# Exp blocks as the weights of the values product, rsqrt as a power on GpSimd, and a new order of the stages, in a fused attention and two-layer kernel

## The chip, the cores and the metric

The kernel runs on one core of a Trainium2 chip. A core has a matrix engine (TensorE, PE in the profile; its weight loads are listed as PEld), VectorE (DVE), ScalarE (ACT), GpSimd (POOL) and SyncE (SP), which here only issues DMAs. Each engine works through its own instructions in order and waits on semaphores for the others. The metric is the device time of one execution in microseconds. Three runs of the kernel before took 408.49, 407.97 and 408.43 us, so its median is 408.43 us. The profile is one further execution.

## The reference

There are 8 batches of 12 heads with 448 positions and 64 features a head. q and k are divided by their root mean square and scaled by g, then attention, then a layer of 2048 units with the "snake" function, then a second layer back to 768:

```python
q_n, k_n = (rmsnorm(q, g_q), rmsnorm(k, g_k))
scores = scale * np.matmul(q_n, k_n.transpose(0, 1, 3, 2))
scores = scores - np.max(scores, axis=-1, keepdims=True)
attn = np.exp(scores)
attn = attn / (np.sum(attn, axis=-1, keepdims=True) + 1e-09)
x = np.matmul(attn, v)            # heads side by side: 3584 x 768
h = x @ w_in                      # 3584 x 2048
s = np.sin(alpha * h)
g = h + s * s / (alpha + 1e-09)
out = g @ w_out                   # 3584 x 768
```

The kernel leaves out the subtraction of the maximum, before and after the change.

## The kernel before

**Stages.** One batch is one stage, and the stages overlap: stage b does the norms, scores, exps and the values product of batch b, then the first product of batch b (`first_product`), and between its steps it does the second product of batch b-1 in small portions called fills (`second_product`, `fill`). After stage 7 the second product of batch 7 is all that is left.

**Chunks and tiles.** A batch's 12 heads are three chunks of four heads. A chunk's scores come in seven tiles (`scores`): four matmuls on four 64x64 quadrants of the array, 448 columns each, into one pair of PSUM banks, and one exp by ACT over 128x896 that writes a bf16 tile `expT`. Keys stand on the partitions, queries on the free axis.

**Order.** Nothing schedules this on its own. Each stage has a plan, a string of tokens, worked off from left to right (`STAGE_0`, `STAGE_1`, and `STAGE_N` for stages 2 to 7), and a second dictionary of tokens that are done beside the first product (`h_plan`). Every engine gets its instructions in the order of the tokens. The tokens, chunk number first: `l` load q and k (two DMAs on SP); `q` squares (by ACT in the first two chunks, else by GpSimd); `u` sum of squares on DVE; `r` one over the root, by a log and an exp on ACT; `g` fold g into q; `k` scale q or k to bf16 (`k30` is chunk 3, q); `t` turn it with two DMA transposes on SP, or `p` with TensorE; `S` a score tile; `V` loads of v; `W` and `O` loads of the weights; `F` or a digit are fills of the second product's current unit, `f` one of the next unit. Chunks 3 to 5 are those of the next batch, 6 and 7 those after it. A fill is two steps of `quadrants` (L538 to L561): eight matmuls on 64x64 quadrants.

**PSUM.** There are four bank pairs. A digit string beside each plan says which pair the next user takes; a user waits until the pair's last reader is done.

**Values product (`attend`, L385 to L441).** v (bf16) is the weight and the exp tile the moving operand, so the result comes out with features on the partitions, ready for the first product. The sums over keys come from matmuls with a weight of ones. Chunk 0 has `o` (ones, halved tiles of 64x32, L404) and `v` (values, 64x64, L416). Chunks 1 and 2 are done together on 64x32 tiles: `x` ones, `y` and `z` the even and odd features. Every tile streams 448 columns, or 224 in the halved ones. The sums are turned into reciprocals by ACT, a log and an exp (L423 to L425, L431, L432), those of chunk 0 are put in place by DVE (L429), and DVE multiplies (L440) into `xT`, the operand of the first product.

**First product (`first_product`, L460 to L496).** 16 row tiles of 128 by six contraction steps kt of 128, 448 columns each (L468), two row tiles to a bank pair. ACT takes the sine (L446), the square is by GpSimd for even tiles (L449) and by ACT for odd ones (L451), DVE adds (L454) into `g_sb` and frees the bank pair.

Of the kernel before, what the change touches and what calls it, by code (L numbers as in the profile page):

```python
# [17 lines left out]
try:  # L18
# [15 lines left out]
        "q000 u000 q010 G q011 q001 u010 g00 u011 r01 g01 D1 u001 k01 r00 k00 q11 u11 O00 q10 V00 p012 "  # L34
        "W01 q20 p00 g1 u10 r1 q21 u20 V01 g2 S4 V02 S k11 l3 k10 S1 S1 S4 W00 W02 S u21 r2 p1 L S2 S q31 "
        "S3 k21 q30 k20 D2 S S3 o3 l4 g3 S W10 W12 o1 o3 p2 u30 l5 S3 u31 S1 S W11 S4 v7 S S S q40 S S x5 "
        "y3 q41 u41 x1 g4 z4 u40 x1 r4 y4 O01 q50 z3 r3 O10 "
    ),
    "012311203203312021021302301231032103021321302",
    {-1: 'u50 O11 k30', 0: 'D4 k401', 1: 'k411', 2: 'q51', 3: 'k31 k400 u51', 5: 'k410', 7: 'g5 V12', 8: 't3 V10 V11 t4 l6 l7'},  # L40
# [3 lines left out]
        "4 r2 f f k20 1 f f 2 k21 S 1 q31 1 t2 S 1 S 2 S q30 2 S 2 S S 3 f S 3 S 1 f S 1 S 1 u31 2 l5 g3 "  # L44
        "S u30 o1 o6 1 r3 V10 2 S f q41 1 f 2 S 2 S 2 q40 S u41 1 v1 v1 S v3 V12 S k31 q50 v2 u40 S 2 S "
        "V11 g5 S z4 x7 y7 r4 z3 g4 k30 "
    ),
    "1320201203203013133213130101301231203123",
    {-1: 'u50 t3', 0: 'k41', 2: 'k40', 5: 'q51', 6: 'l6 t4', 8: 'u51 l7'},
# [3 lines left out]
        "f q40 f 1 f 2 q41 1 S 1 r2 5 f S f f S 2 S 1 u40 k20 1 k21 S 1 u41 1 S 2 S 1 q31 1 o7 1 f f 1 S "  # L53
        "t2 f 1 r4 S 2 f 1 l5 q30 S 3 S 1 u31 1 S 2 u30 g3 V10 S 2 S S k41 3 S v6 r3 k30 S k31 v1 S 2 V12 "
        "g4 2 S 2 S 2 q51 l6 S t3 z3 x7 y5 y2 z4 V11 "
    ),
    "01223131310312323203013012301021310231023",
    {-1: 'k40', 0: 't4', 2: 'q50', 3: 'u50', 4: 'u51 g5', 6: 'l7'},
)
LAST = "0123012"  # L60


def tokens_of(plan):

    return [t for word in plan.split() for t in ("F" * int(word) if word.isdigit() else [word])]
# [3 lines left out]
def kernel(  # L69
# [14 lines left out]

    nc = tc.nc
# [11 lines left out]
    NC = NP // 2  # L105
    SCALE = float(D) ** -0.5
# [8 lines left out]
    vpool = ctx.enter_context(tc.tile_pool(name="vpool", bufs=2))  # L115
    npool = ctx.enter_context(tc.tile_pool(name="norm", bufs=2))
    tpool = ctx.enter_context(tc.tile_pool(name="qkT", bufs=8))
    epool = ctx.enter_context(tc.tile_pool(name="expT", bufs=17))
    hpool = ctx.enter_context(tc.tile_pool(name="parts", bufs=1))
    rpool = ctx.enter_context(tc.tile_pool(name="rec", bufs=2))  # L120
    xpool = ctx.enter_context(tc.tile_pool(name="xT", bufs=1))
# [6 lines left out]

# [3 lines left out]
    upcoming = deque()  # L132
# [11 lines left out]
    qk, vb, norm = {}, {}, {}  # L144

    def strip(pp, hi):

        s = 2 * hi + pp
        return slice(s * 32, s * 32 + 32)

    def half_of(c, pp, hi):

        return pp ^ (hi, 1, 0)[c]

    def load_qk(ci, k_queue=nc.sync):

# [17 lines left out]
    def load_v(b, c):  # L174


        if b not in vb:
            vb[b] = vpool.tile([P, NP, NJ, D], BF16, tag="vb", name="vb")
        heads = v[b].rearrange("(n pp) (p j) d -> n pp p (j d)", pp=2, j=NJ)
        rows = vb[b].rearrange("p n j d -> p n (j d)")  # L180
        if c == 1:
            for r in range(2):
                nc.gpsimd.dma_start(out=rows[r * 64:r * 64 + 64, 1:4], in_=heads[1:4, 1 - r].rearrange("n p x -> p n x"))
        else:
            n = slice(0, 1) if c == 0 else slice(4, NP)
            nc.gpsimd.dma_start(out=rows[:, n], in_=heads[n].rearrange("n pp p x -> (pp p) n x"))
# [7 lines left out]

    load_qk(0, nc.scalar)
# [6 lines left out]
    ones = const.tile([P, D], BF16)  # L202
    nc.vector.memset(ones, 1.0)
    ones_row = const.tile([1, P], F32)
    nc.vector.memset(ones_row, 1.0)
    eps = const.tile([P, 1], F32)
    nc.vector.memset(eps, 1e-6)
    ident = const.tile([P, P], BF16)
# [11 lines left out]
    def spread_g():  # L220

        nc.gpsimd.tensor_mul(g_rows[:, 2], g_rows[:, 0], g_rows[:, 1])
        ps = bank_pair("gps")
        nc.tensor.matmul(ps[:, 0, :D], ones_row, g_rows[:, 2], start=True, stop=True)
        nc.vector.tensor_copy(gg[:, 0], ps[:, 0, :D])
        give_back(ps)

    def spread_alpha():

# [6 lines left out]
    def load_w_in(half, c):  # L236


        cols = slice(half * D_FF // 2, (half + 1) * D_FF // 2)
        rows = moe_w_in[c * 2 * P:(c + 1) * 2 * P, cols]  # L240
        nc.gpsimd.dma_start(out=w_in_sb[half][:, 2 * c:2 * c + 2],  # L241
                            in_=rows.rearrange("(p x) f -> p x f" if c else "(x p) f -> p x f", x=2))

    def load_w_out(hi, lo):
        src = moe_w_out.rearrange("(mt p) d -> p mt d", p=P)
        part = 2 * hi + lo
        mts = slice(part * MT // 4, (part + 1) * MT // 4)
        nc.gpsimd.dma_start(out=w_out_sb[:, mts], in_=src[:, mts])  # L248

    def keep_busy(n, rhs):  # L250


# [7 lines left out]
    def norm_tasks(ci):  # L260

        st = SimpleNamespace()
        early = ci <= NC
        st.ms = npool.tile([P, 2, 2 * NJ], F32, tag="ms", name="ms")
        st.inv, st.inv_ps, st.scaled = {}, [], 0
        st.sq, st.n = {}, None
# [5 lines left out]
        def square(w, heads=(0, 1)):  # L274
            if ci < 2:
                st.sq[w] = spare(2 * ci + w).rearrange("p (a d) -> p a d", d=D)
                rows = slice(heads[0] * NJ, (heads[-1] + 1) * NJ)
                nc.scalar.activation(st.sq[w][:, rows], qk[ci][:, w, rows], ACT.Square)  # L278
            else:
                st.sq[w] = npool.tile([P, 2 * NJ, D], F32, tag="sq", name="sq")  # L280
                nc.gpsimd.tensor_mul(st.sq[w], qk[ci][:, w], qk[ci][:, w])  # L281
# [10 lines left out]
        def rsqrt(ws=slice(0, 2)):  # L292
            ln = npool.tile([P, 2, 2 * NJ], F32, tag="inv", name="inv")
            inv = bank_pair("inv") if early else ln
            if early:
                st.inv_ps.append(inv)
            for w in range(2)[ws]:
                st.inv[w] = inv[:, w, :2 * NJ]
            nc.scalar.activation(ln[:, ws], st.ms[:, ws, :], ACT.Ln, scale=1.0 / D, bias=eps)
            nc.scalar.activation(inv[:, ws, :2 * NJ], ln[:, ws], ACT.Exp, scale=-0.5)  # L300

        def scale(w, heads=(0, 1)):
            eng = nc.vector if early else nc.gpsimd
# [20 lines left out]


# [18 lines left out]
        st.square, st.fold_g, st.reduce, st.rsqrt, st.scale = square, fold_g, reduce, rsqrt, scale  # L344
        st.transpose, st.pe_transpose = transpose, pe_transpose
        return st

    def scores(c, j, warm=0):

# [3 lines left out]
        for pp in range(2):  # L353
            for hi in range(2):
                qkt, r = qkT[2 * c + pp], slice(hi * 64, hi * 64 + 64)
                o = half_of(c % NC, pp, hi) * 64
                nc.tensor.matmul(sc[o:o + 64, hi, :S], qkt[r, 1, j * REST:(j + 1) * REST], qkt[r, 0, :],  # L357
# [5 lines left out]
    avs, recs = {}, {}  # L363
    presums = {}

    def add_tile(b):


        if b not in presums:
            presums[b] = SimpleNamespace(n=0, t=rpool.tile([P, 2, S], F32, tag="rec", name="rec"))  # L370
        s = presums[b]
        first = expT[b * NC, 0] if s.n == 0 else s.t
        s.n += 1
        nc.vector.tensor_add(s.t, first, expT[b * NC, s.n])

    def split_sum(b):

        s = presums[b]
        assert s.n == NJ - 1
        s.parts = [hpool.tile([P, 2, S], BF16, tag=f"part{i}", name="part") for i in range(2)]  # L380
        nc.vector.tensor_copy(s.parts[0], s.t)
        nc.vector.tensor_sub(s.parts[1], s.t, s.parts[0])
# [298 lines left out]
```

The softmax here doesn't subtract the row's maximum and nothing guards it: scores larger than these inputs give would overflow.

## Time and profile before

The profiled execution has a span of 405.8 us from the first to the last instruction; the median of the three timed runs, 408.43 us, is 2.6 us above it.

| | |
|---|---|
| median of three runs | 408.43 us (407.97 to 408.49) |
| span of the profiled execution | 405.8 us |
| stage 0, to the first matmul of a second product | 54.4 us |
| stage 1 | 45.5 us |
| stages 2 to 7, each | 46.8 to 46.9 us |
| after the last first product | 24.5 us |
| score exps on ACT (L360) | 168 x 917 ns |
| squares on GpSimd (L281) | 44 x 1678 ns |
| scaling on GpSimd (L309) | 80 x 938 ns |
| folding g on GpSimd (L286) | 23 x 2098 ns |

How to read it: the times of stages are cut where TensorE passes from line L468 (first product) to line L548 or L529 (second product). A matmul's length in the profile includes its way through the array, some 0.19 us, and consecutive matmuls overlap, so the cost of one in a stream is the distance between starts. "issue" is time in which an engine waited for nothing that the profile shows.

### The profile page before, as it was taken

How to read it: one execution, taken by the hardware profiler on the slowest of the kernel's cores; microseconds unless marked ns; L12 is line 12 of the kernel's file. 1: busy time of each engine (PE TensorE's matmuls, PEld its weight loads, DVE VectorE, ACT ScalarE, POOL GpSimd, SP SyncE). 2: the span in 40 equal slices, each digit the busy share in tenths (PEclk: the TensorE clock that was granted, in tenths of full speed). 3: DMA queues.
4: the chain of work that ended last, by engine and by line, in shares of the span. 5: the costliest groups of instructions: out<-in, count | busy, mean ns of one | idle time of the engine just before them, and what ended most of it. 6: DMA issues, size and time to landing. Idle time of an engine off the chain costs nothing.

```text
span 405.8 us, 15218 instructions
## 1 busy us (share of the span) xinstructions
PE 391.4 (96%) x6755; PEld 238.8 (59%) x6758; DVE 240.6 (59%) x364; ACT 315.3 (78%) x474; POOL 283.6 (70%) x268
## 2 busy tenths in 40 slices
PE   1999999999999999999999999999999999999996
PEld 1346467645675566755676556755667556765564
DVE  4956665756783576638584475836685485544512
ACT  5798889868896879958898678958898679877600
POOL 5998889987959789588877779597895784003300
PEclk9999999999999999999999999999999999999999
DMA  7999999855286925697076923879046901620022
GB/s 266 215 254 241 210 221 255 193 155 171 53 164 162 151 94 88 182 198 153 3 140 178 200 102 70 185 158 209 3 94 179 166 2 22 108 61 1 2 78 79
DMA packets 67846, 55.46 MB, mean 137 GB/s; under 512 B 41524, under 2 KB 63172, under 8 KB 67780
## 3 DMA queue, kind: packets, MB, share of 16 engines
q1 hardware_dynamic: 56578, 41.43, 42.2%
q0 software_dynamic: 10432, 11.81, 19.0%
q8 instruction: 53, 0.87, 0.9%
q10 hardware_dynamic: 770, 1.25, 0.9%
q14 instruction: 13, 0.11, 0.1%
HBM read 45.62 MB, written 11.01 MB: 140 GB/s over the span
## 4 chain that ended last, share of the span: by engine, by line
PE 88%; POOL 5%; DMA 3%; issue 1%; DVE 1%; ACT 1%; SPq 0%; POOLq 0%
PE hps L468 34%; PE ops L548 31%; PE av L416 9%; PE sc L357 7%; PE ops L529 5%; POOL sq L281 2%; DMA qk<-in_q_dram 2%; DMA qk<-in_k_dram 2%; PE av L404 1%; POOL qk L286 1%; POOL w_out_sb L248 1%; POOL w_in L241 1%; ACT expT L360 1%; DVE g_sb L454 0%; DVE xT L440 0%
## 5 line engine op out<-in xcount | busy, mean ns | idle before, releaser
L360 ACT ACTIVATE expT<-sc 128x896 bf16<-128x896 f32 x168 | 143.7, 917 | 7.4 <-PE sc L357 6.6
L548 PE MATMUL ops<-w_out_sb,g_sb 64*64 64x384 bf16 x3072 | 148.0, 323 | 0.0
L468 PE MATMUL hps<-xT,w_in 128*128 128x448 bf16 x768 | 147.0, 353 | 0.4 <-DVE g_sb L454 0.4
L468 PEld LDWEIGHTS <-w_in 128*128 128x128 bf16 x768 | 74.4, 98 | 72.5 <-issue 3.9
L454 DVE SCALAR_TENSOR_TENSOR g_sb<-s,inv_alpha_sb,hps 128x448 bf16<-128x448 f32 x128 | 81.1, 676 | 59.1 <-POOL s L449 58.5
L548 PEld LDWEIGHTS <-g_sb 64*64 64x64 bf16 x3072 | 91.9, 107 | 37.0 <-issue 3.8
L449 POOL TENSOR_TENSOR s<-s 128x448 f32<-128x448 f32 x64 | 59.6, 932 | 65.7 <-ACT s L446 43.9
L446 ACT ACTIVATE s<-hps,alpha_sb 128x448 f32<-128x448 f32 x128 | 73.9, 627 | 37.7 <-PE hps L468 37.2
L309 POOL TENSOR_TENSOR qkn<-qk,inv 128x448 bf16<-128x448 f32 x80 | 72.9, 938 | 24.6 <-issue 17.1
L281 POOL TENSOR_TENSOR sq<-qk 128x896 f32<-128x896 f32 x44 | 73.3, 1678 | 3.9 <-DVE ms L290 3.0
L357 PE MATMUL sc<-qkT 64*64 64x448 bf16 x672 | 60.3, 357 | 0.7 <-ACT expT L360 0.3
L286 POOL TENSOR_TENSOR qk<-qk,gg 128x896 f32<-128x896 f32 (+1 forms) x25 | 50.5, 2021 | 2.2 <-ACT g_sb L278 1.5
L554 DVE COPY osb<-ops 128x384 f32<-128x384 f32 x48 | 26.7, 556 | 38.5 <-PE ops L548 38.3
L290 DVE TENSOR_REDUCE ms<-sq 128x14 f32<-128x896 f32 x44 | 46.4, 1078 | 3.3 <-POOL sq L281 3.2
L440 DVE TENSOR_TENSOR xT<-av,rec 128x896 bf16<-128x896 f32 (+1 forms) x26 | 25.7, 1016 | 26.8 <-ACT rec L432 21.4
L451 ACT ACTIVATE s<-s 128x448 f32<-128x448 f32 x64 | 36.9, 577 | 2.9 <-DVE g_sb L454 0.7
L416 PE MATMUL av<-expT,vb 64*32 64x448 bf16 (+1 forms) x1120 | 38.1, 350 | 0.0
L357 PEld LDWEIGHTS <-qkT 64*64 64x64 bf16 x672 | 21.7, 107 | 13.8 <-issue 6.7
L555 DVE TENSOR_TENSOR osb<-osb,ops 128x384 f32<-128x384 f32 x48 | 26.6, 554 | 1.7
L416 PEld LDWEIGHTS <-vb 64*32 64x32 bf16 (+1 forms) x1120 | 20.8, 96 | 11.0 <-issue 2.2
L429 DVE TENSOR_REDUCE rec<-rec 32x448 f32<-32x448 f32 x28 | 17.1, 610 | 9.7 <-ACT rec L425 9.4
L529 PE MATMUL ops<-w_out_sb,g_sb 128*128 128x384 bf16 (+1 forms) x144 | 21.0, 309 | 0.0
(51 smaller groups left out, 185.8 us busy)
## 6 DMA issues: line engine op xcount, KB each, us to landing
qk<-in_q_dram SPq DMA_DIRECT2D x23, 448.0 KB, 5.2
qk<-in_k_dram SPq DMA_DIRECT2D x23, 448.0 KB, 5.7
out_dram<-osb SPq DMA_DIRECT2D x45, 192.0 KB, 2.9
w_out_sb<-in_moe_w_out_dram POOLq DMA_DIRECT2D x4, 768.0 KB, 12.8
w_in<-in_moe_w_in_dram POOLq DMA_DIRECT2D x6, 512.0 KB, 12.2
vb<-in_v_dram POOLq DMA_DIRECT2D x16, 168.0 KB, 7.2
vb<-in_v_dram POOLq DMA_DIRECT2D x8, 224.0 KB, 5.3
out_dram<-osb SPq DMA_DIRECT2D x13, 96.0 KB, 4.3
```

Source lines behind the costliest of these rows:

```text
L281: nc.gpsimd.tensor_mul(st.sq[w], qk[ci][:, w], qk[ci][:, w])
L286: nc.gpsimd.tensor_mul(x, x, gg.to_broadcast([P, len(heads) * NJ, D]))
L290: nc.vector.reduce_sum(st.ms[:, w, rows], st.sq[w][:, rows], axis=AX.X)
L309: eng.tensor_mul(n[:, :, hi, :], x[:, hi], inv[:, hi].unsqueeze(2).to_broadcast([P, NJ, D]))
L357: nc.tensor.matmul(sc[o:o + 64, hi, :S], qkt[r, 1, j * REST:(j + 1) * REST], qkt[r, 0, :], start=True, stop=True)
L360: nc.scalar.activation(expT[c, j], sc[:, :, :S], ACT.Exp, scale=SCALE)
L416: nc.tensor.matmul(av[o, k, :S], w, x[r, hi, :], start=(j == 0), stop=(j == last))
L446: nc.scalar.activation(s1, hps, ACT.Sin, scale=alpha_sb[:, m, :])
L449: nc.gpsimd.tensor_mul(s2, s1, s1)
L454: nc.vector.scalar_tensor_tensor(g_sb[:, m, (b % 2) * S:(b % 2 + 1) * S], s2, inv_alpha_sb[:, m, :], hps, op0=ALU.mult, op1=ALU.add)
L468: nc.tensor.matmul(ps[:, m % 2, :S], w_in_sb[m * 2 // MT][:, kt, m % (MT // 2) * P:(m % (MT // 2) + 1) * P], x[:, kt, :], start=(kt == ORD ...
L548: nc.tensor.matmul(st["ps"][os, r, :HALF], g_sb[rs, m, c0 + o * 64:c0 + o * 64 + 64], w_out_sb[rs, m, half * HALF:(half + 1) * HALF], star ...
```

## The change

**Values product (`values` in place of `attend`).** The exp tile becomes the weight and v the moving operand. The tile `v_ones` holds v in bf16 with a column of ones behind the 64 features of each head and key block, so that 65 columns stream and the 65th result is the sum over the keys. Queries now come out on the partitions. For each chunk and each of six exp tiles there are six matmuls on the whole array (128 queries, 128 keys) and, where a block of 128 queries straddles two heads, two on half the columns (128x64); the seventh exp tile takes 28 matmuls on 64x64 quadrants. `scores` lays the keys out to suit. DVE then takes the reciprocals of the sums straight from PSUM (14 a partition) and multiplies into `xn`, a bf16 tile. The logs and exps of the sums on ACT and the moves on DVE are gone.

**Turn.** `xn` has queries on the partitions, the first product wants features there. `T` turns a chunk with one DMA transpose on SP; `P` does it with seven transposes on TensorE and a copy by ACT or DVE. Stage 0 has three `P`, stage 1 `T0 T1 P21`, the others `T0 T1 T2`.

**v.** It is loaded in f32 into one buffer, half by DMAs from SP and half from GpSimd in most stages, and cast to `v_ones` by DVE (`C`) or GpSimd (`c`).

**rsqrt.** `w` computes it on GpSimd: a multiply and add, then a power of -0.5. `r` and `R` remain for some chunks. `q` and `Q` now say who squares, and in stages 1 to 7 some squares go to ACT.

**First product.** `H` opens a bank pair in the plan itself: two row tiles on kt 0 to 3. Two of them are opened; kt 4 and 5 (chunk 2) follow in `first_product`.

**Order.** All plans are new, and one string `SLOTS` gives the bank pairs of the whole kernel. There are 14 exp tiles in place of 17. w_out is loaded by column halves, and batch 0's second product does all first halves before the second ones. The numbers of score tiles, fills and first-product matmuls are unchanged.

```diff
@@ plans (the end of STAGE_N, before and after)
-        "f q40 f 1 f 2 q41 1 S 1 r2 5 f S f f S 2 S 1 u40 k20 1 k21 S 1 u41 1 S 2 S 1 q31 1 o7 1 f f 1 S "
-        "t2 f 1 r4 S 2 f 1 l5 q30 S 3 S 1 u31 1 S 2 u30 g3 V10 S 2 S S k41 3 S v6 r3 k30 S k31 v1 S 2 V12 "
-        "g4 2 S 2 S 2 q51 l6 S t3 z3 x7 y5 y2 z4 V11 "
-    {-1: 'k40', 0: 't4', 2: 'q50', 3: 'u50', 4: 'u51 g5', 6: 'l7'},
+        "f f 1 f 4 q41 S 1 f S 1 f 3 q31 w2 S 1 S u31 3 V111 1 k20 S V10 1 u41 S S q30 3 f f S f S f S k21 f "
+        "f 1 S 1 u30 f f 1 q40 u40 S v7 t2 S g4 w3 2 S T0 1 R4 1 S 1 S v7 S 1 k40 2 S 1 T1 f g3 S k30 f 1 S 2 "
+        "l5 f k41 f S Q51 v7 f q50 f f T2 2 g5 H k31 l7 c11 C12 l6 t4 H u50 t3 "
+    {
+        1: "C10",
+        5: "u51",
+    },
@@ rsqrt on GpSimd
+        def rsqrt_pow(ws):
+            inv = npool.tile([P, 2, 2 * NJ], F32, tag="inv", name="inv")
...
+            nc.gpsimd.tensor_scalar(out=inv[:, ws], in0=st.ms[:, ws], scalar1=1.0 / D, scalar2=1e-6, op0=ALU.mult, op1=ALU.add)
+            nc.gpsimd.tensor_tensor(out=inv[:, ws], in0=inv[:, ws], in1=minus_half.unsqueeze(2).to_broadcast([P, len(range(2)[ws]), 2 * NJ]), op=ALU.pow)
@@ values product
-    def attend(b, what, tiles=range(NJ)):
...
+    def values(b, c, js):
+        if js[0] == 0:
+            avs[b, c] = bank_pair("av")
+        av = avs[b, c]
+        es = {j: expT.pop((b * NC + c, j)).rearrange("p hi s -> p (hi s)") for j in js}
+        for whole in (True, False):
+            for j in js:
+                if j == NJ - 1:
+                    continue
+                pp, k = divmod(j, NK)
+                for i in range(NJ):
+                    if (i == NJ // 2) == whole:
+                        continue
+                    for o in range(1 if whole else 2):
+                        hi = o if i == NJ // 2 else i // (NJ // 2 + 1)
+                        n = P if whole else 64
+                        q0 = i * P + o * 64
+                        nc.tensor.matmul(av[o * 64:o * 64 + n, pp, i * W:(i + 1) * W], es[j][:, q0:q0 + n],
+                                         v_ones[b % 2][:, 4 * c + 2 * hi + pp, k], start=(k == 0 and i == 0), stop=False)
...
+                    nc.tensor.matmul(av[o * 64:o * 64 + 64, pp, i * W:(i + 1) * W], es[NJ - 1][r, pos * 64:pos * 64 + 64],
+                                     v_ones[b % 2][r, 4 * c + 2 * (pos // NJ) + pp, NK], start=False, stop=(i == NJ - 1))
+        sums = av[:, :, :NJ * W].rearrange("p pp (i w) -> p pp i w", w=W)
+        rec = npool.tile([P, 2, NJ, 1], F32, tag="rec", name="rec")
+        nc.vector.reciprocal(rec, sums[:, :, :, D:])
+        xn[b, c] = npool.tile([P, NJ, 2, D], BF16, tag="xn", name="xn")
+        nc.vector.tensor_mul(xn[b, c].rearrange("p i pp d -> p pp i d"), sums[:, :, :, :D], rec.to_broadcast([P, 2, NJ, D]))
+        give_back(avs.pop((b, c)))
@@ turn, cast, opening of the first product
+    def turn(b, c):
+        x = xT[b, c] = xpool.tile([P, 2, S], BF16, tag="xT", name="xT")
+        nc.sync.dma_start_transpose(out=x.rearrange("p k s -> p (k s)").rearrange("p (i t) -> p i t", t=P),
+                                    in_=xn.pop((b, c)).rearrange("p i pp d -> p (i pp d)"))
...
+    def cast_v(b, c, eng):
+        heads = slice(4 * c, 4 * c + 4)
+        eng.tensor_copy(v_ones[b % 2][:, heads, :, :D].rearrange("p h s d -> p (h s) d"),
+                        v_raw[:, heads].rearrange("p h s d -> p (h s) d"))
...
+    def open_product(b):
+        i = len(opened)
+        opened[i] = bank_pair("hps")
+        for m in (2 * i, 2 * i + 1):
+            multiply(b, i, m, range(KT - 2))
```

In the prediction, tokens are named as in the plans: `v7` is a values product of one chunk, `T2` the DMA turn of chunk 2, `H` an opened pair, `k21` the scaling of chunk 2's k, `c11` and `C12` casts for the next batch.

## The prediction, made before the changed kernel ran

> **What bounds the kernel now.** I read the page's busy shares first, then a cut by stage at the instants at which TensorE passes from the first product of one batch to the second, then the chain that ended last, then the groups, and last single stretches of the timeline. The busy shares, and two rows of the 40 slices:
>
> ```profile
> PE 391.4 (96%) x6755; PEld 238.8 (59%) x6758; DVE 240.6 (59%) x364; ACT 315.3 (78%) x474; POOL 283.6 (70%) x268
> ...
> PE   1999999999999999999999999999999999999996
> ...
> PEclk9999999999999999999999999999999999999999
> ```
>
> TensorE is busy throughout at full clock; nobody else is over 78%. The cut by stage (stretch, its length, then busy time of PE, PEld, DVE, ACT, POOL, clock, DMA share, GB/s):
>
> ```profile
> 0.00:54.40 54.40, 43.78 (x515) 22.09 (x518) 36.36 (x62) 42.62 (x69) 45.80 (x52) 1.00 1.06 234
> 54.40:99.90 45.50, 45.23 (x821) 28.37 (x820) 27.18 (x41) 38.83 (x58) 41.32 (x38) 1.00 0.84 207
> 99.90:146.80 46.90, 46.90 (x881) 29.05 (x880) 30.37 (x45) 38.91 (x58) 36.90 (x33) 1.00 0.69 135
> 146.80:193.70 46.90, 46.90 (x881) 29.36 (x880) 29.21 (x44) 38.80 (x58) 36.87 (x33) 1.00 0.63 135
> ```
>
> The six stages on STAGE_N take 46.92 us each and TensorE is never idle in them, so each lasts as long as its matmuls stream. Stage 0 waits for loads and norms, stage 1 has about 1 us of gaps, the tail after the last first product is 24.5 us. The chain that ended last agrees: it is TensorE for 88%.
>
> ```profile
> PE 88%; POOL 5%; DMA 3%; issue 1%; DVE 1%; ACT 1%; SPq 0%; POOLq 0%
> ```
>
> So the question is what the change does to a stage's TensorE time, and whether the new order still hides everything else. What its pieces cost, from the timeline of TensorE (start, length, line, tile rows*columns, operand, count):
>
> ```profile
> 17.52 0.89 PE L334 MATMUL tp<-ident,qkn 64*128 64x64 bf16 x28
> ...
> 109.04 0.82 PE L548 MATMUL ops<-w_out_sb,g_sb 64*64 64x384 bf16 x16
> 109.79 0.86 PE L404 MATMUL av<-expT,ones 64*32 64x224 bf16 x56
> 110.58 0.68 PE L548 MATMUL ops<-w_out_sb,g_sb 64*64 64x384 bf16 x12
> ```
>
> A length includes about 0.19 us until the last result is out. Taking that off, 28 transposes of 64 columns, each with new weights of 128 columns, go at 26 to 29 ns; four concurrent quadrant matmuls of 384 columns take 163 ns (0.65 us per 16 in the chain), a score tile of 448 columns 189 ns, eight 64x32 tiles of 224 columns 96 ns. That is columns/2.4 plus 2 ns. At 109.79 and 110.58 the tile shape changes, and about 94 ns are lost each time beyond the streaming of the last group.
>
> [...] transposes issued right behind two loads took up to 10.5 us, alone 3.1 to 3.3:
>
> ```profile
> L319 SPq DMA_TRANSPOSE qkT<-qkn x42: 1228/1315/3583, 49.6 to 345.5; - x42
> ...
> DMA to landing us min/median/max: 3.1/4.8/10.5
> ```
>
> **The change part by part**, for one STAGE_N stage.
>
> *Values product, TensorE.* Removed: 7 halved ones steps at 96 ns (0.67) and 28 steps at 189 ns (ones and values of the old three groups, 5.29), and three shape changes (0.28): 6.24 us. Added per chunk: 36 matmuls 128x128 on 65 columns at 29 ns (1.05); 12 of 128x64 in 6 pairs and 28 of 64x64 in 7 fours. At streaming rate these are 29 ns each (0.17 + 0.20); [...]. So 1.43 to 1.77, I take 1.5. Plus three shape changes per `v7` (into whole, into half, into quadrants), 0.28. Three chunks: 5.34. Net -0.90 us a stage, bounds -1.1 to -0.1. Fills (56), score tiles (21) and the first product's 96 matmuls are the same in number.
>
> *The last turn, `T2`, is the new wait.* After the last `v7`, TensorE has three fills (0.98), two more (0.65), a shape change (0.09) and two `H` with 16 matmuls at 0.189 (3.02): 4.74 us of cover. Then the matmuls on kt 4 and 5 need xT of chunk 2. Its way: last result 0.2, reciprocal 0.25 (the 128x16 one took that), multiply 1.09 (row L440, same shape), three handoffs 0.15: SP issues at 1.7. A transpose alone lands 3.1 to 3.3 later: 4.8 to 5.0. I put the wait at 0.3. On TensorE the whole first product stands behind this wait, and ACT's sines behind that. Ahead of `T2` on SP is `T1`, then `l5` some 4 us earlier; loads take 5.2 and 5.7 us to land, so they are just out of its way. `T0` and `T1` have over 6 us. Queued behind `T2` on SP are two stores, `l7`, `l6`, `t4`, `t3`: they are wanted only at the next stage's scores, some 17 us on.
>
> *ACT* (38.9 us busy a stage) loses the logs and exps of the sums (0.54+0.58+0.58+0.92+0.95) and two of three rsqrt pairs (1.1), gains a square (0.94): worth nothing, TensorE hides it. *DVE* exchanges its three multiplies and four 0.61 us moves for three multiplies with a 0.25 us reciprocal and two casts of 1024 elements (1.2 each, scaled from the reduce of 896 at 1.08, L290): 29.2 to about 29.9, hidden. *GpSimd* (36.9): one square less (1.68), two V issues less (1.3), a cast more [...], two small multiply-adds (0.2 each) and two powers of 128x28. No row shows a power: at least 0.3 (the 1x64 multiply), at most I allow 3; I take 0.7. Sum 36.7 of 46, hidden on the whole. Two places are close, in us from the stage's start. (a) GpSimd begins at 1.7, as before, with `q41`, `q31` (3.3), `w2` (0.9), a V load (1.3), `k20` (1.8), `q30` (1.7), `k21` (1.8): 12.5; the first transpose of `t2` lands 3.1 to 4.5 later, at 15.7 to 17.1, and TensorE, by the sum of its pieces, comes to chunk 2's first scores at 17.1. So a power may take 0.7 to 2 before the scores wait. (b) `l5` goes out behind `T1` at 22.6 and its q lands at 27.8; `q50`, `g5`, `k31` and the cast end 6.6 later, at 34.4, then the first square of the snake (0.93) and two of its sums on DVE (1.35): the first bank pair is free at 36.7. TensorE wants it for the fifth pair of the first product at 30.6 + 0.3 + 1.5 + 2 x 2.26 = 36.9. I add 0.1 for both and for the eleventh exp, whose bank pair the first `v7` takes at 13.6, just as it comes free (exps in a row go at 0.83 us). V in f32 by SP reads the same bytes.
>
> A stage: 46.92 - 0.90 + 0.3 + 0.1 = 46.4. Six: -3.0. *Stage 1* (45.5): the same -0.9, plus 7 whole transposes for `P21` (0.4), minus some 0.2 of its gaps: -0.7. *Stage 0*: ACT and GpSimd trade squares, rsqrt and log/exp, sums near equal; first product opened before the last turn: -0.4, give or take 2. *Tail*: same. Sum -4.1 on the profiled execution's 405.8 us gives 401.7; the median of the runs is 2.6 above that span, so 404.3.
>
> **Rivals.** *`T2` lands late (slower).* The median transpose took 4.8 us, not 3.2. Then it lands at 6.6 against 4.74, 1.8 us of TensorE idle in each of six stages in place of 0.3: +9.0 on the forecast, 413. It decides from a wait of about 1.0 us, a latency near 4 us. For: 32 of 42 transposes took over 4. Against: the slow ones stood right behind loads or a store, `T2` doesn't. *Weights don't hide.* If a 128-row load with 65 columns costs 56 ns, 36 x 27 ns x 3 = 2.9 us more a stage, with stage 0 and 1 some +22: 426. Against: the transposes' 29 ns. *The power is dear.* At 3 us, `t2` is 2 us late and the stage ends later by as much: about 413; the profile says nothing on it. *It doesn't do what it says*: the small tiles at 56 ns eat the gain; 408.
>
> **How the numbers follow.** Likeliest, at 404.3 (own range 401 to 407): 0.57. Better still, small tiles at streaming rate and stage 0 shorter, 399 to 401: 0.07. Gain eaten, 407 to 409: 0.13. `T2` late 0.11, power 0.06, weights 0.06, together 409.3 and up: 0.23. A measurement here tells 0.2% (0.8 us) from no change. Faster 0.69, same 0.09, slower 0.22. Range 400 to 412.5.
>
> **What would show it.** The stages on STAGE_N should be 46.0 to 46.8 long; values matmuls on whole tiles 29 ns apart; TensorE idle before kt 4 of the first product by 0 to 0.6 us, put down to the turn's DMA; scores never waiting for GpSimd. A power over 2 us, whole values matmuls over 40 ns apart, or over 1 us of idle before kt 4 would make the forecast wrong.

## The result, and the profile after

The changed kernel takes 458.25 us in the median (457.2 to 460.37) against 408.46 us for the kernel before (the three runs above and a fourth): 1.1237 times as long, 95% interval 1.1191 to 1.1282. Its profiled execution has a span of 456.0 us, 50.2 more than the one before. The first line of the page and the chain that ended last:

```profile
PE 403.3 (88%) x6623; PEld 249.6 (55%) x6623; DVE 251.3 (55%) x373; ACT 299.3 (66%) x422; POOL 335.8 (74%) x278
...
POOL 39%; PE 34%; issue 12%; DVE 9%; DMA 3%; ACT 2%; SPq 0%; POOLq 0%; ACTq 0%
```

TensorE carried 88% of the chain before, now 34%; GpSimd carries the most. The cut by stage, columns as before (stretch, length, then busy time of PE, PEld, DVE, ACT, POOL, clock, DMA share, GB/s):

```profile
0.00:74.90 74.90, 52.70 (x548) 26.95 (x550) 48.56 (x65) 45.07 (x64) 57.91 (x59) 0.86 0.96 199
74.90:122.00 47.10, 45.26 (x800) 29.25 (x799) 27.86 (x42) 39.21 (x58) 31.39 (x29) 1.00 0.90 207
122.00:174.20 52.20, 46.95 (x857) 30.08 (x857) 30.53 (x46) 35.80 (x51) 46.23 (x36) 1.00 0.69 148
174.20:227.70 53.50, 48.51 (x857) 30.25 (x856) 29.23 (x45) 35.90 (x50) 45.78 (x35) 0.97 0.68 144
...
385.00:431.20 46.20, 46.20 (x857) 29.89 (x857) 21.79 (x37) 34.35 (x47) 16.10 (x14) 1.00 0.28 57
```

So the 50.2 us are: stage 0 +20.4, stage 1 +1.7, stages 2 to 6 +28.4 together (5.0 to 6.6 each), stage 7 -0.7, tail +0.3. Stage 7, which prepares no next batch and gives GpSimd only 16.1 us of work, is *faster* than before (46.8), with TensorE never idle. Of the groups (busy time, mean ns, idle before and its releasers):

```profile
L304 POOL TENSOR_TENSOR inv<-inv,minus_half 128x28 f32<-128x28 f32 x14 | 67.3, 4804 | 1.2
L386 PE MATMUL av<-v_ones,expT 128*128 128x65 bf16 (+1 forms) x1152 | 39.4, 197 | 0.1
L313 DVE TENSOR_TENSOR qkn<-qk,inv 128x448 bf16<-128x448 f32 x16 | 19.3, 1256 | 9.0 <-POOL inv L304 7.9 <-ACT inv L296 0.9 <-issue 0.2
L178 DVE CAST v_ones<-v_raw 128x1024 bf16<-128x1024 f32 x14 | 11.4, 812 | 2.9 <-DMA v_raw<-in_v_dram 2.9
L178 POOL CAST v_ones<-v_raw 128x1024 bf16<-128x1024 f32 x10 | 10.6, 1063 | 0.0
```

A power of 128x28 takes 4.80 us on GpSimd. What it replaces, a log and an exp on ACT, took 0.31 and 0.22 us in the kernel before:

```profile
L299 ACT ACTIVATE inv<-ms,eps 128x28 f32<-128x28 f32 x23 | 7.2, 313 | 2.2 <-DVE ms L290 2.2
L300 ACT ACTIVATE inv<-inv 128x28 f32<-128x28 f32 x23 | 5.1, 222 | 0.8
```

And the 16 scalings of the early chunks on DVE, 0.61 us each before (L309), take 1.26 in the mean. Where GpSimd's time goes in stage 3 (174.2 to 227.7), from its timeline:

```profile
175.97 3.32 POOL L276 TENSOR_TENSOR sq<-qk 128x896 f32<-128x896 f32 x2
179.37 0.21 POOL L303 TENSOR_SCALAR inv<-ms 128x28 f32<-128x28 f32 x1
179.67 4.79 POOL L304 TENSOR_TENSOR inv<-inv,minus_half 128x28 f32<-128x28 f32 x1
...
195.23 4.81 POOL L304 TENSOR_TENSOR inv<-inv,minus_half 128x28 f32<-128x28 f32 x1
...
213.58 1.04 POOL L178 CAST v_ones<-v_raw 128x1024 bf16<-128x1024 f32 x1
214.57 1.83 POOL L428 TENSOR_TENSOR s<-s 128x448 f32<-128x448 f32 x2
```

From 175.97 to the first squares of the snake the timeline lists not one gap. What that does to TensorE, from its timeline of the same stage (in brackets the idle time before the piece, and what ended it):

```profile
191.49 0.38 PE L360 MATMUL sc<-qkT 64*64 64x448 bf16 x4 [1.47 <-DVE osb L537]
194.59 0.38 PE L360 MATMUL sc<-qkT 64*64 64x448 bf16 x4 [1.23 <-DMA qkT<-qkn]
216.87 1.51 PE L445 MATMUL hps<-xT,w_in 128*128 128x448 bf16 x5 [2.28 <-DVE g_sb L433]
```

The second is the wait of chunk 2's scores for their transposes. The first is the same lateness by another way: DVE's moves of the second product (L537) stand behind its reduce (L285), which waits 4.48 us for a late square. The third is the fifth pair of the first product, which waits until the snake has freed a bank pair. That is 4.98 us of idle time in all. In stages 3 and 5 the granted clock of TensorE also fell, to 0.50 at the lowest, for some 3 us after the third wait (2.28 and 2.07 us; 0.97 in the mean of each stage): the 48 matmuls behind it take 10.93 and 10.92 us, and TensorE is busy for 48.5 and 48.6 us of the stage where stage 2 has 47.0. In stages 2, 4 and 6 (waits of 1.08, 2.15 and 2.02) the clock stayed at 1.00 and they take 9.24. In stage 0, with 0.86 in the mean, the last 48 matmuls of the first product take 10.71. This slower clock is a part of the 50.2 us.

### The profile page after: what moved, and what is told of

Read it like the earlier page. It is cut to its first block, busy times and chain, and to the rows that moved or that the text cites. A ratio compares the mean times of both kernels' runs of the same rounds, so it can differ in the third digit from the quotient of the medians.

```text
span 456.0 us, 15025 instructions
## 1 busy us (share of the span) xinstructions
PE 403.3 (88%) x6623; PEld 249.6 (55%) x6623; DVE 251.3 (55%) x373; ACT 299.3 (66%) x422; POOL 335.8 (74%) x278
## 4 chain that ended last, share of the span: by engine, by line
POOL 39%; PE 34%; issue 12%; DVE 9%; DMA 3%; ACT 2%; SPq 0%; POOLq 0%; ACTq 0%
PE hps L445 17%; POOL qkn L313 12%; POOL sq L276 9%; PE ops L529 7%; POOL inv L304 6%; POOL qk L281 5%; PE ops L512 5%; DVE qkn L313 4%; POOL s L428 3%; DVE g_sb L433 3%; DMA qk<-in_k_dram 2%; PE sc L360 2%; PE av L386 2%; DVE ms L285 2%; DMA qkT<-qkn 1%
## 5 line engine op out<-in xcount | busy, mean ns | idle before, releaser
L363 ACT ACTIVATE expT<-sc 128x896 bf16<-128x896 f32 x168 | 145.4, 917 | 60.2 <-PE sc L360 59.5
L445 PE MATMUL hps<-xT,w_in 128*128 128x448 bf16 x768 | 153.3, 360 | 13.2 <-DVE g_sb L433 12.7
L428 POOL TENSOR_TENSOR s<-s 128x448 f32<-128x448 f32 x64 | 61.8, 969 | 71.6 <-ACT s L425 49.2
L360 PE MATMUL sc<-qkT 64*64 64x448 bf16 x672 | 63.3, 373 | 16.9 <-DVE osb L537 7.7
L313 POOL TENSOR_TENSOR qkn<-qk,inv 128x448 bf16<-128x448 f32 x80 | 73.5, 944 | 1.9 <-issue 1.3
L304 POOL TENSOR_TENSOR inv<-inv,minus_half 128x28 f32<-128x28 f32 x14 | 67.3, 4804 | 1.2
L285 DVE TENSOR_REDUCE ms<-sq 128x14 f32<-128x896 f32 x44 | 46.9, 1080 | 36.8 <-POOL sq L276 36.8
L276 POOL TENSOR_TENSOR sq<-qk 128x896 f32<-128x896 f32 x28 | 48.7, 1745 | 2.4 <-DMA qk<-in_k_dram 2.4
L386 PEld LDWEIGHTS <-expT 128*128 128x128 bf16 (+1 forms) x1152 | 35.2, 102 | 9.4 <-issue 6.5
L386 PE MATMUL av<-v_ones,expT 128*128 128x65 bf16 (+1 forms) x1152 | 39.4, 197 | 0.1
L430 ACT ACTIVATE s<-s 128x448 f32<-128x448 f32 x64 | 36.9, 577 | 3.2 <-DVE g_sb L433 0.5
L399 DVE RECIPROCAL rec<-av 128x14 f32<-128x14 f32 x24 | 5.8, 243 | 45.6 <-PE av L395 45.6
L537 DVE TENSOR_TENSOR osb<-osb,ops 128x384 f32<-128x384 f32 x48 | 26.6, 554 | 1.7
L274 ACT ACTIVATE sq<-qk 128x896 f32<-128x896 f32 x16 | 15.0, 952 | 18.7 <-DMA qk<-in_k_dram 18.7
```

Of the source, the lines that this page charges most:

```text
L276: nc.gpsimd.tensor_mul(st.sq[w][:, rows], x, x)
L304: nc.gpsimd.tensor_tensor(out=inv[:, ws], in0=inv[:, ws], in1=minus_half.unsqueeze(2).to_broadcast([P, len(range(2)[ws]), 2 * NJ]), op=ALU ...
L313: eng.tensor_mul(n[:, :, hi, :], x[:, hi], inv[:, hi].unsqueeze(2).to_broadcast([P, NJ, D]))
L360: nc.tensor.matmul(sc[o * 64:o * 64 + 64, hi, :S], qkt[r, 1, key * REST:(key + 1) * REST], qkt[r, 0, :], start=True, stop=True)
L363: nc.scalar.activation(expT[c, j], sc[:, :, :S], ACT.Exp, scale=SCALE)
L386: nc.tensor.matmul(av[o * 64:o * 64 + n, pp, i * W:(i + 1) * W], es[j][:, q0:q0 + n], v_ones[b % 2][:, 4 * c + 2 * hi + pp, k], start=(k = ...
```

## The experiments

**Theory.** The power costs 4.8 us. Two of them in a middle stage fill GpSimd, three in stage 0 stand on its chain. **Rivals.** The new values product, its turns and its order cost TensorE the time; or, in stage 0, something else that came along does. In stage 0 two rivals of the power turn up below: where the inverse lies, and the order of the bank pairs. One table for all, from the profiled executions (us; "mid" is the mean of stages 2 to 6, POOL is GpSimd's busy time in stage 3):

| kernel | whole, median | ratio to before (95%) | stage 0 | stage 1 | mid | POOL |
|---|---|---|---|---|---|---|
| before | 407.5 to 408.5 | | 54.4 | 45.5 | 46.9 | 36.9 |
| changed | 458.25 | 1.124 (1.119 to 1.128) | 74.9 | 47.2 | 52.6 | 45.8 |
| A no power, ACT's log and exp | 414.57 | 1.017 (1.012 to 1.022) | 59.3 | 48.0 | 46.9 | 35.9 |
| B as A, early inverses in PSUM | 417.34 | 1.022 (1.017 to 1.028) | 63.8 | 47.5 | 46.8 | 35.9 |
| C before, two powers a stage | 434.50 | 1.066 (1.062 to 1.070) | 55.4 | 54.4 | 50.4 | 46.9 |
| D changed, powers halved | 462.04 (one run) | | 73.5 | 48.9 | 53.3 | 46.5 |
| E power w2 alone | 429.61 | 1.051 (1.049 to 1.054) | 57.6 | 50.1 | 49.9 | 40.9 |
| F power w3 alone | 415.75 | 1.017 (1.015 to 1.019) | 59.6 | 48.5 | 46.8 | 40.9 |
| G w2 and w3, none early | 442.02 | 1.083 (1.078 to 1.088) | 59.6 | 46.9 | 52.6 | 45.8 |
| H as A, Q21 moved | 413.54 | 1.013 (1.010 to 1.016) | 58.5 | 48.0 | 46.7 | 35.9 |
| I as A, one inverse in PSUM | 415.75 | 1.018 (1.014 to 1.022) | 59.6 | 49.2 | 46.5 | 35.9 |
| J before, early inverses in SBUF | 415.85 | 1.018 (1.014 to 1.021) | 63.4 | 45.8 | 46.9 | 36.9 |
| K as B, other order, l5 earlier | 415.36 | 1.018 (1.014 to 1.023) | 59.4 | 49.6 | 46.8 | 35.8 |
| L changed, early inverses copied to PSUM | 454.07 | 1.112 (1.107 to 1.116) | 72.3 | 49.2 | 52.2 | 45.7 |

The stage times are of one execution each. Stages 0 and 1 are the same code in A, E, F and G, and they take 57.6 to 59.6 and 46.9 to 50.1 us. A smaller difference between two kernels in these stages tells nothing.

### A: no power

```diff
-nc.gpsimd.tensor_scalar(out=inv[:, ws], in0=st.ms[:, ws], scalar1=1.0 / D, scalar2=1e-6, ...)
-nc.gpsimd.tensor_tensor(out=inv[:, ws], in0=inv[:, ws], in1=minus_half..., op=ALU.pow)
+nc.scalar.activation(inv[:, ws], st.ms[:, ws], ACT.Ln, scale=1.0 / D, bias=eps)
+nc.scalar.activation(inv[:, ws], inv[:, ws], ACT.Exp, scale=-0.5)
```

> The changed kernel with every GpSimd power (and its multiply-add) replaced by the logarithm and exp of ACT into the same SBUF tile; order of work, loads and values product untouched. Theory (two powers of 4.8 us make GpSimd the bound of a middle stage, three lengthen stage 0): GpSimd falls from 45.8 to about 36 us a middle stage, the middle stages from 52-53.5 to 46.0-46.8, stage 0 from 74.9 to 56-64, the whole from 458 to 405-415. The early scalings on DVE stay at 1.2 us or so if the place of the inverse (SBUF) slows them, and fall to 0.6 if the power beside them did. Rival (the new values product, the turns and the order on TensorE cost the time): middle stages stay at 51-53, the whole above 445.

43.7 of the 49.8 us are gone with this edit alone. Its cut by stage, stages 0, 1, 3 and 4:

```profile
0.00:59.26 59.26, 47.58 (x540) 25.40 (x545) 40.99 (x64) 45.50 (x70) 43.11 (x53) 1.00 1.10 243
59.26:107.29 48.03, 45.00 (x800) 29.70 (x799) 28.49 (x43) 39.31 (x59) 31.84 (x30) 1.00 0.95 214
...
154.56:200.99 46.43, 46.38 (x859) 29.67 (x858) 30.31 (x45) 36.26 (x54) 35.87 (x31) 1.00 0.85 165
200.99:247.42 46.43, 46.33 (x857) 29.78 (x856) 30.10 (x45) 36.36 (x54) 35.89 (x31) 1.00 0.75 167
```

Two middle stages take 46.43 us, the other three 47.0 to 47.3, so 46.9 in the mean, as before the change. The rival that the values product and the order cost the time in them is out. What stays is 4.8 us in stage 0 and 2.6 in stage 1 (3.2 to 5.2 and 1.4 to 4.6 in the four runs of the same code).

### C and D: the power by itself

C puts powers into the kernel before, for two of three chunks from the last one of batch 1 on, and changes nothing else:

```diff
+            if ci >= NC + 2 and ci % NC != 1:
+                nc.gpsimd.tensor_scalar(...)      # as in the change
+                nc.gpsimd.tensor_tensor(..., op=ALU.pow)
+                return
```

> The kernel before with the rsqrt of two chunks in three, from the last chunk of batch 1 on, computed by GpSimd's multiply-add and power in place of ACT's logarithm and exp; nothing else. Theory: each power takes 4.8 us, GpSimd goes from 36.9 to about 46.9 us of a 46.9 us stage, so the scores, the snake's squares or the scalings come late and the middle stages lengthen by 1 to 6 us each; the whole 413-440. Rival (the power costs only in the new order, with its work for the values on GpSimd): the whole within 3 us of 408.

Slower by 6.6%, without any of the new order. Chain and power, from its page:

```profile
POOL 43%; PE 27%; DVE 10%; issue 7%; ACT 5%; DMA 5%; SPq 0%; POOLq 0%; ACTq 0%
...
L303 POOL TENSOR_TENSOR inv<-inv,minus_half 128x28 f32<-128x28 f32 x13 | 62.5, 4809 | 1.1
```

The middle stages are 50.2 to 51.3 with GpSimd busy for 46.9 of them, stage 1 is 54.4. D cuts each power into q's half and k's half:

```diff
-nc.gpsimd.tensor_tensor(out=inv[:, ws], in0=inv[:, ws], ..., op=ALU.pow)
+for w in range(2)[ws]:
+    nc.gpsimd.tensor_tensor(out=inv[:, w:w + 1], in0=inv[:, w:w + 1], ..., op=ALU.pow)
```

> The changed kernel with each power cut in two, one of 128x14 for q and one for k. If a power's time goes by the element, 2.4 us each and the whole within 3 us of 458. If it is mostly fixed (a call, a table), 4 to 4.8 each, GpSimd takes about 9 us more a middle stage, and the whole is 500 or above.

```profile
L305 POOL TENSOR_TENSOR inv<-inv,minus_half 128x14 f32<-128x14 f32 x28 | 72.1, 2589 | 1.2
```

2.59 us for 14 columns, 4.80 for 28: an estimate from these two sizes is 0.158 us a column and 0.38 fixed. By it, most of the price goes by the element. The whole, in its one run, is 1.0 us beyond the range that was expected.

### E, F and G: which power

The edit of A for some chunks only. In each the early chunks go to ACT.

```diff
+            if ci > 3 and ci % NC == 2:      # E, w2; in F ci % NC == 0, w3; in G ci > 3 alone
                 nc.gpsimd.tensor_scalar(...)
                 nc.gpsimd.tensor_tensor(..., op=ALU.pow)
+            else:
+                nc.scalar.activation(inv[:, ws], st.ms[:, ws], ACT.Ln, ...)
+                nc.scalar.activation(inv[:, ws], inv[:, ws], ACT.Exp, scale=-0.5)
```

> The changed kernel with one power a middle stage: that of the chunk whose transposed q and k the stage's own last scores need (w2) stays on GpSimd; the other (w3) and the three of stages 0 and 1 go to ACT's logarithm and exp. GpSimd should be at 40.9 us a middle stage. If GpSimd's sum is what binds (45.8 of work and a few waits between), one power is hidden by the 5.5 us left: middle stages 46.4-47.5, the whole 413-418. If it is the place (what stands behind the power on GpSimd is due at once), this one still makes the last scores late by 1 to 3 us: middle stages 48-50, the whole 421-430.

> The other way round: the power of the next batch's first chunk (w3) stays on GpSimd, that of w2 goes to ACT. By the sum: middle stages 46.4-47.5, the whole 413-418, as with the other power alone. By the place: nothing in this stage's scores stands behind it, only the snake's first sums do, so the middle stages are 46.5-48.5, with the idle time of TensorE before its fifth pair of the first product and none before the scores; the whole 414-422.

> The changed kernel with the powers of the middle stages (w2 and w3) on GpSimd and the three of the early chunks by ACT's logarithm and exp. If the two places of loss add up, stage 0 is 57.5-59.6 as without any power, the middle stages 52-53.5 as in the changed kernel, the whole 441-445. With one power a stage the middle stages were 49.5 (w2) and 46.8 (w3), so both together should show whether they add (49.8) or more (52-53.5), which would mean that the second one falls on a GpSimd that has no time left.

E, TensorE's timeline in stage 4:

```profile
225.76 0.38 PE L364 MATMUL sc<-qkT 64*64 64x448 bf16 x4 [1.50 <-DVE osb L541]
229.01 0.38 PE L364 MATMUL sc<-qkT 64*64 64x448 bf16 x4 [1.38 <-DMA qkT<-qkn]
```

F, the same view, where stage 3 has only this:

```profile
192.70 9.24 PE L449 MATMUL hps<-xT,w_in 128*128 128x448 bf16 x48 [0.32 <-DVE g_sb L437]
```

The same 4.8 us on the same engine, with 40.9 us of work for GpSimd both times, cost 3.0 us a stage in one place and nothing in the other. `w2` stands before the scaling and transposes that this stage's scores wait for; behind `w3` stands only what the snake's first squares wait for, and there GpSimd had time to spare. In A's stage 3 it stands idle for 4.8 us between `w3`'s place and those squares, which the power fills:

```profile
173.39 1.84 POOL L313 TENSOR_TENSOR qkn<-qk,inv 128x448 bf16<-128x448 f32 x2 [3.31 <-ACT inv L296]
...
182.45 1.68 POOL L276 TENSOR_TENSOR sq<-qk 128x896 f32<-128x896 f32 x1 [1.47 <-DMA qk<-in_q_dram]
```

Both powers together cost 5.7, not 3.0: the second one uses up what the first had left, and the wait of 2.28 us before the fifth pair appears on top. G adds up: stage 0 as in A, middle stages as in the changed kernel. So I had to give up "GpSimd's sum binds" as the whole account: with one power the place decides, with two the sum as well.

### J, L and B: where the inverse lies

In the kernel before, DVE read the early chunks' inverses from PSUM; `w` leaves them in SBUF. The prediction did not look at this. J does that to the kernel before, and for chunk 0 too, whose inverse the changed kernel leaves in PSUM (`r`):

```diff
-                st.inv[w] = inv[:, w, :2 * NJ]
+                st.inv[w] = ln[:, w]
...
-            nc.scalar.activation(inv[:, ws, :2 * NJ], ln[:, ws], ACT.Exp, scale=-0.5)
+            nc.scalar.activation(ln[:, ws], ln[:, ws], ACT.Exp, scale=-0.5)
```

> The kernel before, with one thing changed: the inverses of the early chunks (0 to 3), which DVE multiplies by, are read from SBUF and not from a PSUM bank pair (the pair is still taken and given back, so the order of the bank pairs is as it was). If the place of the inverse is what lets GpSimd's work stall DVE's scaling, some of the 16 scalings of stage 0, those beside a GpSimd multiply or square, take 1.2 to 3 us in place of 0.61, those beside DMA issues alone stay at 0.61; stage 0 grows by 0.5 to 4 us and the whole is 408-412. If the stalls belonged to the new order or to the powers, all 16 stay at 0.61 and the whole within 0.8 us of 408.

It costs 1.8%: stage 0 is 8.9 us longer, over twice what I allowed, and the 16 scalings take 11.7 us more in sum (1.345 us in the mean against 0.612). The scalings of the kernel before (min/median/max in ns), then of J:

```profile
L309 DVE TENSOR_TENSOR qkn<-qk,inv x16: 561/615/622, 8.3 to 49.0; 128x448 bf16<-128x448 f32 x16
```

```profile
L309 DVE TENSOR_TENSOR qkn<-qk,inv x16: 610/616/7956, 8.5 to 58.0; 128x448 bf16<-128x448 f32 x16
```

One of them, of chunk 0, starts at 10.40 and takes 7.96 us. DVE and GpSimd in J at that time:

```profile
10.40 7.96 DVE L309 TENSOR_TENSOR qkn<-qk,inv 128x448 bf16<-128x448 f32 x1
...
10.74 0.70 POOL L241 DMA_DIRECT2D w_in<-in_moe_w_in_dram  x1
11.45 1.69 POOL L281 TENSOR_TENSOR sq<-qk 128x896 f32<-128x896 f32 x1
13.09 2.07 POOL L286 TENSOR_TENSOR qk<-qk,gg 128x896 f32<-128x896 f32 x1
15.12 1.67 POOL L281 TENSOR_TENSOR sq<-qk 128x896 f32<-128x896 f32 x1
16.74 1.31 POOL L183 DMA_DIRECT2D vb<-in_v_dram  x2
18.06 2.23 POOL L286 TENSOR_TENSOR qk<-qk,gg 128x896 f32<-128x896 f32 x1
```

In the kernel before, the scalings from 14.31 to 16.51 ran beside the same multiply and square at 0.61 each. In J the six that take over 0.7 us (0.74 to 7.96) all stand beside GpSimd arithmetic; the four at 22 to 24 us, beside none, take 0.61. So in J it took both: the inverse beside the other operand in SBUF, and arithmetic of GpSimd, whose operands lie in SBUF too. The longest scaling began while GpSimd issued a DMA, 1.05 us before its square at 11.45, and yet ended behind that square, a multiply and a second square. Why, the profile does not show.

What the stalls cost the changed kernel J does not measure: its longest one is on chunk 0, which the change leaves in PSUM. In the changed kernel the scalings take 10.3 us more in sum than before (1.256 us in the mean of the 16), all on chunks 1 to 3; in A, with the same inverses in SBUF but no power, 3.7 (0.844).

L asks what that is worth in the changed kernel: powers kept, and DVE copies the early inverses into a bank pair.

```diff
+            if ci <= NC:
+                ps = bank_pair("inv", oldest=True)
+                nc.vector.tensor_copy(ps[:, ws, :2 * NJ], inv[:, ws])
```

> The changed kernel with all its powers; only the inverse of the early chunks (1 to 3) is moved by DVE from SBUF into a PSUM bank pair before the scalings read it there. Stage 0 of the changed kernel is 20.4 us longer than before's; the powers replaced by ACT took 15.6 of it away, but that also changed what ran beside the scalings. If the stalls of DVE's scalings (3.2, 2.5, 2.5 and 2.1 us beyond 0.61 each in the changed kernel) are a part of their own, all 16 take 0.6 us here and stage 0 falls from 74.9 to 66-71, the whole to 449-454. If a stalled scaling only fills time in which the next power is awaited anyway, stage 0 stays at 73-76 and the whole at 456-460.

```profile
L321 DVE TENSOR_TENSOR qkn<-qk,inv x16: 610/614/623, 8.4 to 56.0; 128x448 bf16<-128x448 f32 x16
```

No scaling stalls any more. Stage 0 falls by 2.6 us, to 72.3, between the two cases, and the whole to 1.112 of the kernel before, where the changed kernel has 1.124. What the stalls cost by themselves this does not say. The 2.6 us are little more than the scatter, stage 1 is 2.0 longer than in the changed kernel, the mean clock of stage 0 is 0.98 in place of 0.86, and the inverse now holds a bank pair: TensorE waits 6.5 us for the scaling of chunk 1 and has then computed two score tiles fewer than the changed kernel at this point. But the powers are the larger part of stage 0: taking them out as well brought it down by 15.6 (A), moving the inverses by 2.6.

B is A with the inverses in PSUM, in the bank pair that comes free first, out of the written order:

```diff
+            ln = npool.tile([P, 2, 2 * NJ], F32, tag="inv", name="inv")
+            early = ci <= NC
+            inv = bank_pair("inv", oldest=True) if early else ln
...
```

> As the one before, and the inverses of the early chunks lie in a PSUM bank pair, as in the kernel before, in place of SBUF. Theory (DVE's scaling is slowed by the inverse in SBUF while GpSimd works): the early scalings take 0.6 us each in place of 1.2 to 1.8, stage 0 is a further 3 to 8 us shorter, the middle stages are the same as in the run before, the whole 398-406. Rival (the place of the inverse is nothing): stage 0 and the whole within 1 us of the run before.

The scalings were at 0.61, as expected, and stage 0 was 4.6 us *longer* than in A; the forecast of 398 to 406 fails. Either a pair is now missing for the scores, or the order of the pairs is bad; K tells.

### H, I and K: what is left of stage 0 and stage 1

H is A with one token of stage 0 moved; I is B for one chunk alone.

```diff
-... u11 Q21 p012 p00 Q20 ...
+... u11 p012 p00 Q21 Q20 ...
```

```diff
-            early = ci <= NC      # B
+            early = ci == 2       # I
```

> The changed kernel without powers (as in the first of these runs), and in stage 0 ACT's square of chunk 2's k (token Q21) is moved behind the two moves out of PSUM (p012 and p00), which stood behind it while it waited for its load. If this order is part of the 4.8 us by which stage 0 stays longer than in the kernel before, stage 0 falls from 59.3 to 57.5-58.8; if not, it stays at 59 to 60.

> The changed kernel without powers, with the inverse of chunk 2 alone in a PSUM bank pair and those of chunks 1 and 3 in SBUF. The four scalings of chunk 2 on DVE should take 0.6 us each in place of 2.63 and 0.61 x3. If that stall of 2 us is part of what stage 0 is longer by, it falls from 59.3 to 57-58.5; if taking a bank pair out of turn costs as much, as it seems to have with three of them, it stays at 59 or goes to 61.

H's 58.5 and I's 59.6 tell nothing beside the scatter of stage 0 (57.6 to 59.6), though I's scalings of chunk 2 did take 0.61 to 0.62 us. K puts things together: Q21 moved, inverses in PSUM, stage 0's bank pairs oldest first, and in stage 1 the load `l5` before `T1`.

```diff
-"S 1 S T0 f f f 1 S S V111 2 f S 2 S 1 v7 T1 S 1 S 1 l5 1 g4 ..."
+"S 1 S T0 f f f 1 S S V111 2 f S 2 S 1 l5 v7 T1 S 1 S 1 1 g4 ..."
```

> The changed kernel without powers, with Q21 behind the two moves, the inverses of all early chunks in PSUM, the bank pairs of stage 0 taken oldest first in place of the written order, and in stage 1 the load l5 ahead of the turn T1. If what the PSUM inverses cost before was the order of the bank pairs, stage 0 falls from 58.5-59.5 to 55-57.5; if it is that a pair is missing, it stays at 59 or above (63.8 with them out of turn). If stage 1's 1.2 us before the fifth pair of the first product come from l5's late landing, they go, and stage 1 falls from 47.9-48.5 to 46.5-47.3. The middle stages stay at 46.4-47.2, the whole 406-413.

With the bank pairs oldest first stage 0 is 59.4 in place of B's 63.8, so most of what B lost belongs to their order. (K also moves Q21, for which H showed no more than the scatter.) But stage 0 gains nothing over A, though no scaling stalls in K; its expectation had put "59 or above" down to a missing pair, which no run shows by itself. In stage 1 of K, from TensorE's timeline:

```profile
90.26 1.30 PE L452 MATMUL hps<-xT,w_in 128*128 128x448 bf16 x6 [1.58 <-DMA xT<-xn]
...
99.86 1.48 PE L452 MATMUL hps<-xT,w_in 128*128 128x448 bf16 x7 [0.34 <-DVE g_sb L440]
```

The wait before the fifth pair fell from A's 1.20 to 0.34, as expected. That does not show that moving `l5` did it: in B, E and I, where `l5` stands as in A, this wait is 0.30 or 0.31. In these three and in K TensorE lost 1.06 to 1.58 us just before, among the first eight matmuls of the first product; in A, F, G and H it lost nothing there and waits 1.09 to 1.21 at the fifth pair. What is lost before is not lost again. K lost it to `T1`, which, now right behind two loads on SP, took 7.2 us to land. Its stage 1 is 49.6, not the 46.5 to 47.3 expected.

The other three lost it in a pause for which the profile shows no cause ("issue"). In stage 1 such pauses take 0.97 us in A, 1.07 in F and 3.4 in E, where there are three; G has none. G's stage 1 is the shortest with 46.9 us, E's the longest with 50.1.

No version here beats the kernel before. A middle stage without powers is at best 0.5 us shorter (46.43), which would be 2.9 over six stages; A gains 0.8 over its six. Stages 0 and 1 together lose 6.6 to 9.1 without early powers, and 11.5 in B. What makes up the 3 to 5 us that stage 0 keeps without any power stays open. ACT is busy for 45.5 us of it against 42.6, since the new plan gives it squares that the powers were to make room for; that this is the cause was not tried.

## Why the prediction was wrong

**The term that failed** is in the sum for GpSimd: "No row shows a power: at least 0.3 (the 1x64 multiply), at most I allow 3; I take 0.7." It is 4.80. I took the price of a multiply of 64 elements for the lower end and a round number for the upper; nothing in the profile bears on the second, nor on the 0.7. The sum of 36.7 became 45.8; without the powers A has 35.9, where my own terms give 34.9. "Hidden on the whole" was then wrong by 5.7 us a stage. The rival "the power is dear" had the mechanism and place right, with 0.06 of the chance, and stopped at 3 us. An unknown operation that runs twice a stage should have carried the range to where it fills its engine. By my terms GpSimd had 11 us to spare without the powers, 5.5 for each; at (a), with 0.7 to 2 free, a power of 5.5 makes a stage 3.5 to 4.8 us longer, an estimate of 425 to 433 for the whole.

**The two close places were right, the reasons in part.** At (a) I wrote that a power may take 0.7 to 2 before the scores wait; with 4.8 they wait 2.9 in E's stage 4 (1.50 and 1.38), so that 1.9 was to be had. Of these, only the 1.38 is the wait for transposes that I had in mind; the 1.50 came by a place that I missed, DVE's reduce, which waits for a late square and holds up the moves of the second product behind it. At (b), the first bank pair of the snake, TensorE waits 2.28 us. I had it depend on when `l5` lands; in the changed kernel it is GpSimd's queue, without a gap up to there.

**Stage 0**, "sums near equal ... -0.4, give or take 2", measured +20.4. I compared the engines' sums where a chain binds. On it stand powers (A: 15.6 away with them and with part of the stalls), scalings that stall because the inverse left PSUM (10.3 us in sum; their share of the stage is not settled), and 3 to 5 us that stay open. That `w` moves the inverse to SBUF was in the diff; I did not read it for that, and no view of before shows what it costs.

**Stage 1**, -0.7, measured +1.7. I read about 1 us of gaps in the stage before, where the cut has 45.23 busy of 45.50. A shows three idle spells: 0.79 before a move of DVE, 0.97 inside a group of fills that nothing in the profile explains, and 1.20 at (b), which K does not settle. G, without such a pause, is still 1.4 longer than the kernel before.

**Right:** in A's stage 3 whole values matmuls start 29 ns apart mostly, 31 in the mean, so the rival on weights is out. The quadrant tiles did not take 56 ns either: in the same stage seven groups of four take 0.24 us up to the next piece, 34 ns each. (Those 56 ns, in two rivals and behind the 1.77 and the -0.1, were the author's estimate; no view of before shows them.) Reciprocal 0.24 (0.25), turn's multiply 1.09 (1.09), multiply-add 0.21 (0.2), cast on DVE 0.81 (1.2), on GpSimd 1.06 (the 1.0 in the sum of 36.7 was the author's estimate, from no row). `T2` did not bind, so that rival is out too: no wait for it shows in the changed kernel, and 0.21 us once in A. Where the trace has its landing, it took 2.9 to 3.2 us, as forecast. (Of the transposes before, the trace has the landing of 34, and 27 of them took over 4 us, not 32 of 42.)

**Right by luck:** the best middle stages without powers take 46.43, and I had 46.4. But the values product saves less than my 0.9. In A's stage 3, from TensorE's timeline:

```profile
168.13 0.38 PE L360 MATMUL sc<-qkT 64*64 64x448 bf16 x4
168.44 1.58 PE L386 MATMUL av<-v_ones,expT 128*128 128x65 bf16 x48
169.95 0.42 PE L395 MATMUL av<-v_ones,expT 64*64 64x65 bf16 x28
170.19 0.37 PE L360 MATMUL sc<-qkT 64*64 64x448 bf16 x4
```

From its first matmul to the next piece a chunk takes 1.75 us, and before the first stands a change of shape: 0.31 from the score tile, which streams for 0.19, so 0.12 more. (A length on the page is 0.16 us more than the distance between two starts, 353 against 189 ns in the first product of the kernel before, and not 0.19; what that is made of no view shows.) The three chunks of the stage, taken so, come to 5.7 against my 5.34, a saving of 0.5. The 0.3 that I added for `T2` was not needed, and the two errors nearly cancel.

## What to carry to other kernels

When an operation has no row in the trace, find out how many of it fill its engine's idle time and let the range reach there; an upper end that "feels" generous is no bound. Price a moved operation by what stands behind it: the same 4.8 us cost 3.0 us ahead of the transposes that the scores need, nothing ahead of the snake, and 5.7 when both were there. And when an edit changes where an operand lies, look at what else works on that memory at the time: in J one scaling took 7.96 us in place of 0.61.

## What the runs showed of the hardware

A power of f32 operands on GpSimd took 4.80 us for 128x28 and 2.59 for 128x14 (D): by an estimate from these two, 0.158 for each column of 128 partitions and 0.38 more.

A multiply of DVE of 128x448 with both inputs in SBUF, 0.61 us beside no arithmetic of GpSimd, took up to 7.96 while GpSimd worked through several instructions (J); with one input in PSUM it stayed at 0.61 beside the same multiply and square (the kernel before).

And TensorE pauses now and then in the middle of a group for nothing that the profile shows: 0.97 us among A's fills in stage 1, 2.28 within four score matmuls of K. Behind stage 0, all such pauses of one run are a multiple of 128 matmuls apart, counted in the trace: E's stand before its 862nd, 1118th and 1246th matmul, A's before the 1114th and 1754th, F's before the 1118th and 4318th. A run has three of them at most, the kernel before none. What happens every 128 matmuls no run here shows.
